# Freed input tiles as output buffers, and a new order for the last head, in a gated attention and MLP backward kernel

## The chip, the cores and the metric

The kernel runs on one core of one Trainium2 chip. The metric is the device time of one execution in microseconds (us). Engines are named as in the profile: PE (TensorE matmul), PEld (its weight load), DVE (VectorE), ACT (ScalarE), POOL (GpSimd) and SP (SyncE, which here only issues transfers). The core has 16 DMA engines, over which a transfer is spread.

## The reference

One decode step of attention over a cache (32 heads, 4096 keys, head size 128) and an MLP are mixed by a gate; the kernel returns the output and the gradients of nine inputs, in bf16.

```python
def _A_ref(x, k_cache, v_cache, wq, wo):           # D = 640
    q = (x @ wq).reshape(B, Sq, H, Dh).transpose(0, 2, 1, 3)
    scores = jnp.einsum("bhqd,bhkd->bhqk", q, k_cache) * (Dh ** -0.5)
    p = _softmax(scores, axis=-1)
    o = jnp.einsum("bhqk,bhkd->bhqd", p, v_cache)
    return o.transpose(0, 2, 1, 3).reshape(B, Sq, H * Dh) @ wo

def _B_ref(x, w1, b1, w2):                         # F = 1728
    h = jnp.einsum("bsd,df->bsf", x, w1) + b1
    sp = jnp.log1p(jnp.exp(-jnp.abs(h))) + jnp.where(h > 0, h, jnp.zeros_like(h))
    return jnp.einsum("bsf,fd->bsd", h * jnp.tanh(sp), w2)

g = _sigmoid((x * gate_w).sum(-1, keepdims=True))
out = g * _A_ref(x, ...) + (1 - g) * _B_ref(B_x, ...)
_out, _vjp = jax.vjp(_f, A_x, A_k_cache, A_v_cache, A_wq, A_wo, B_w1, B_b1, B_w2, gate_w)
return (_out, *_vjp(grad_out))
```

With one query per head, dV of a head is the outer product of p (4096) and do (128), and dK that of ds and the scaled q. So every head reads 1 MB of K and 1 MB of V and writes 1 MB of dV and 1 MB of dK: 128 MB of the 164.6 MB that the kernel moves.

## The kernel before

**Tiles.** A head's K or V is one tile of 128 partitions x 4096 bf16 (`Kn`, `Vn`, 1 MB each; KBUFS = VBUFS = 4 buffers of each). A dV or dK is built in a tile `o_sb` of the same shape, of which there are four. Weights of wq come in pairs of head groups (`wq_p`, 1280 KB), those of wo by group (`wo_g`, 640 KB); w1 and w2 stay in SBUF as a whole (`w1_sb`, `w2_sb`, both `w_sb` in the profile). dWq, dWo, dW1 and dW2 are written over these tiles and stored from there. w2 has 1728 rows: 1664 lie in 13 columns of 128 partitions, the last 64 in column FR, on 64 partitions; its gradient `out_8` is stored in three transfers of the 13 columns (L787) and one of the 64 rows (L788).

**The loop.** `for h in range(H - 1)` (L729) runs heads in a pipeline written out by hand: while head h is finished, K and V of h + 1 are transposed on PE (`k_pe`, `v_pe`, L506) and copied out by ACT (L515, through `ev()`), and scores of h + 1 are made (`k_rows`, `v_rows`). `softmax` finds the maximum, `exps` the exponential (ACT, L566), `pjs` and `zd_mm` the sums, `probs` p and ds (DVE). `dv_out` and `dk_out` build the outer products on DVE in two halves (L589, each 128 x 2048) and store them from SP's queue (L602). `dq_o` has PE read the natural K and V once more (L617) for dq and o of the head; `dqo_red` collects these one head later from what `rw_cp` (ACT) and `x_tr` (PE) bring. It is the last use of Kn and Vn of that head, behind which `load_k(h + 4)` and `load_v(h + 4)` are issued while h + 4 < 32, for the last time at h = 27.

**Groups.** Four heads share a group of weights. At the first head of the next group (hh = 0) the sums of a group are closed: `f_diag`, `f_bc` and `l_dqbf` prepare dq, `l_pe` multiplies it with the transposed wq (`w_pe("q", ...)`, L324, copied by ACT, L330) and o with wo; `f_dwo` writes dWo on ACT (L374), `f_dwq` writes dWq on DVE (L366).

**Queues.** Each engine runs its instructions in the order of the program. All large transfers stand in SP's queue: a store there holds back whatever stands behind it until its data are there. At h = 28 (H - 4) the stores of dW2 are put in, at h = 30 (H - 2) those of db1 and dW1 (L791 to L793). ACT issues four small loads at the start and two stores of `fin_rows` at the end (L906, L908); POOL issues some small ones.

**After the loop** (L840 on) comes head 31: its softmax; `dqo_red(30)`; the sums over three heads of the last group; twenty transposes of wq; `probs`; the second half of dK of 30; `dq_o`; the closing of the group; dWq (DVE, and ACT by `l_dwq`, L361) and its store; dWo on ACT and its store; the end of the small outputs, with dV of 31 in their middle; and dK of 31 as the last thing.

Of the kernel before, what the change touches and what calls it, by code (L numbers as in the profile page):

```python
# [8 lines left out]
ALU = mybir.AluOpType  # L9
# [7 lines left out]
def kernel(  # L17
# [24 lines left out]
    nc = tc.nc  # L42
# [239 lines left out]
    def f_new(g):  # L282
        gp = groups[g]
        gp["o_bf"] = grp_sb.tile([P, G], BF16, name="o_bf", tag="o_bf")
        gp["dq_bc"] = grp_sb.tile([P, GD], BF16, name="dq_bc", tag="dq_bc", bufs=1)
# [9 lines left out]
    def f_bc(g, a=0, b=G):  # L295
        g_bcast(groups[g]["dq_diag"], groups[g]["dq_bc"], a, b)

    def f_o4(g):
        gp = groups[g]
        gp["o4_ps"] = grp([P, G], F32, "o4_ps")  # L300
        nc.tensor.matmul(gp["o4_ps"][:], lhsT=gp["o_sel"][:].rearrange("p h k -> p (h k)"), rhs=res[:],
                         start=True, stop=True)
# [11 lines left out]
    def w_pe(kind, g, k):  # L314
        n = min(TB, G * RC - k * TB)
        tp = tr_ps.tile([P, TB, P], BF16, name="tr", tag="tr")
        for t in range(n):
            if kind == "q":
                hh, c = divmod(k * TB + t, RC)
                src = wqs[g][:, c, hh * Dh:(hh + 1) * Dh]  # L320
            else:
                c, hh = divmod(k * TB + t, G)
                src = wos[g][:, hh, c * P:(c + 1) * P]
            nc.tensor.transpose(tp[:, t, :], src, ident_bf[:])  # L324
        trq.append(lambda: w_ev(kind, g, k, n, tp))
# [27 lines left out]
    def l_add(g, slot, o):  # L353
        ax = groups[g]["ax"]
        if o:
            nc.vector.tensor_tensor(aT_acc[:], aT_acc[:], ax[:, 0, :], ALU.add)
        nc.vector.tensor_copy(dx_parts[:, :, slot], ax[:, 1, :])
# [15 lines left out]
    def f_dwo(g, hh):  # L373
        nc.scalar.activation(wos[g][:, hh, :], da_bc[:], ACT.Copy, scale=groups[g]["o4"][:, hh:hh + 1])  # L374

    def f_dwo_st(g):
        nc.sync.dma_start(dwo4_v[g], wos[g][:])

# [130 lines left out]
    def ev():  # L509
        trq.pop(0)()  # L510
# [27 lines left out]
    def rw_cp(h):  # L538
        rw_sb[h] = small.tile([P, 4, P], F32, name="rw_sb", tag="rw_sb", bufs=1)
        nc.scalar.copy(rw_sb[h][:].rearrange("p t r -> p (t r)"), rw[:])  # L540

    def x_tr(h):
        t = rw_sb.pop(h)
        xs[h] = s_ps.tile([P, 4, P], F32, name="x", tag="x")
        for j in range(4):
            nc.tensor.transpose(xs[h][:, 3 - j, :], t[:, j, :], ident_f[:])  # L546
        v = xs[h][:].rearrange("p t r -> p (t r)").rearrange("p (j u) -> p j u", u=16)
        sd[h] = (v[:, :, 4], v[:, :, 5])
# [19 lines left out]
    def pjs(h):  # L568
        pj = small.tile([P, J], F32, name="pj", tag="pj", bufs=2)
        nc.vector.scalar_tensor_tensor(pj[:], in0=sd[h][1], scalar=1.0, in1=es[h][:],  # L570
                                       op0=ALU.mult, op1=ALU.mult, accum_out=zds[h][:, 1:2])

    def zd_mm(h, mx):
        nc.tensor.matmul(mx[:, P:P + 2], lhsT=ones_f[:], rhs=zds[h][:], start=True, stop=True)  # L574
# [21 lines left out]
    def out_half(w, h, dst, col4, row, k):  # L596
        hh = h % G
        if k == 0:
            o_t[w, h] = outs.tile([P, J, Dh], BF16, name="o_sb", tag="o_sb")
        outer(o_t[w, h], col4, row[:, hh * Dh:(hh + 1) * Dh], k * JH, (k + 1) * JH)  # L600
        if k == 1:
            nc.sync.dma_start(dst[h], o_t.pop((w, h))[:])  # L602
# [4 lines left out]
    def dk_out(h, k):  # L607
        if h >= 0:
            out_half("k", h, dKv, ds4s[h], groups[h // G]["qs_row"], k)
# [12 lines left out]
    def dqo_red(h, x):  # L622
        if h >= 0:
            v = x[:].rearrange("p t r -> p (t r)")[:, 3:3 + 4 * (P - 1)].rearrange("p (s q) -> p s q", q=P - 1)
            nc.vector.tensor_reduce(groups[h // G]["dqo"][:, :, h % G],
                                    v[:, :, 0:P - 1:32].rearrange("p s (i c) -> p i s c", i=2),
                                    axis=AX.XY, op=ALU.add)
# [101 lines left out]
    for h in range(H - 1):  # L729
        g, hh = h // G, h % G  # L730
        nx, pv = g + 1 < NG, g > 0
        k_pe(h + 1, 2)
        ev()
        mx, negM = softmax(h)
        if hh == 3 and nx:
            g_qpair_cp(g + 1)
            g_docol(g + 1)
        dqo_red(h - 1, xs[h])
        k_pe(h + 1, 3)
        ev()  # L740
        exps(h, negM)
        dk_out(h - 1, 1)
        v_pe(h + 1, 0)
        if hh == 2 and nx:
            g_q(g + 1)
        v_pe(h + 1, 1)
        if hh == 3 and nx:
            g_dopair(g + 1)
            g_dopair_cp(g + 1)
        k_rows(h + 1)  # L750
        ev()
        ev()
        pjs(h)
        v_pe(h + 1, 2)
        ev()
        zd_mm(h, mx)
        if hh == 0 and pv:
            f_new(g - 1)
            l_new(g - 1)
            l_dqbf(g - 1, 0, G)  # L760
            f_diag(g - 1)
        elif h >= 2:
            mlp_some(0.9, False)
        v_pe(h + 1, 3)
        ev()
        probs(h, mx)
        if hh == 0 and pv:
            f_o4(g - 1)
            f_o4c(g - 1)
            f_bc(g - 1)  # L770
        dv_out(h, 0)
        k_pe(h + 2, 0)
        dq_o(h)
        v_rows(h + 1)
        rw_cp(h + 1)
        if h + 2 < H:
            ev()
        dv_out(h, 1)
        load_k(h + KBUFS)
        load_v(h + VBUFS)  # L780
        k_pe(h + 2, 1)
        if h + 2 < H:
            ev()
        if h == H - 4:
            assert dw2_next[0] == FCN
            for a, b in W2P:
                nc.sync.dma_start(dw2_v[:, a:b, :], w2_sb[:, a:b, :])  # L787
            nc.sync.dma_start(out_8[FM:F, :], w2_sb[0:FT, FR, :])  # L788
        if h == H - 2:
            assert not mq  # L790
            nc.sync.dma_start(db1_row, dh_bc[0:1, :])  # L791
            nc.sync.dma_start(dw1_v[:, 0:3, :], w1_sb[:, 0:3, :])
            nc.sync.dma_start(dw1_v[:, 3:RC, :], w1_sb[:, 3:RC, :])  # L793
        dk_out(h, 0)
        x_tr(h + 1)
        maxes(h + 1)
        if hh == 0:
            if nx:
                g_new(g + 1)
            if pv:  # L800
                l_pe(g - 1, 0, G)
                wT.pop(("q", g - 1))
                l_add(g - 1, g - 1, True)
                for t in range(G):
                    f_dwo(g - 1, t)
                f_dwo_st(g - 1)
                f_dwq(g - 1, 0)
                f_dwq(g - 1, 1)
        if hh == 1:
            if pv:  # L810
                for c in range(2, RC):
                    f_dwq(g - 1, c)
                f_dwq_st(g - 1)
            if nx:
                w_pe("o", g + 1, 0)
                ev()
                w_pe("o", g + 1, 1)
                ev()
        if hh == 2:
            if g + 2 < NG:  # L820
                load_wo(g + 2)
            if nx:
                w_pe("o", g + 1, 2)
                ev()
                g_do(g + 1)
                g_qcol(g + 1)
                g_qpair(g + 1)
        if hh == 3:
            if g % 2 == 0 and g + 4 <= NG:
                load_wqp(g // 2 + 1)  # L830
            if nx:
                g_qs(g + 1)
                for k in range(NWT):
                    w_pe("q", g, k)
                    ev()
        if h >= 2:
            mlp_some(0.9 if hh < 2 else 1.8)
            dw2_some(2)
# [6 lines left out]
    mx, negM = softmax(h)  # L845
    exps(h, negM)
    dqo_red(h - 1, xs[h])
    f_new(g)
    l_new(g)
    f_diag(g, 0, 3)  # L850
    l_dqbf(g, 0, 3)
    pjs(h)
    zd_mm(h, mx)
    f_bc(g, 0, 3)
    for k in range(NWT):
        w_pe("q", g, k)
        ev()
    l_pe(g, 0, 3)
    probs(h, mx)
    dk_out(h - 1, 1)  # L860
    dq_o(h)
    rw_cp(H)
    l_add(g, g, False)
    x_tr(H)
    dqo_red(h, xs[H])
    f_diag(g, 3, 4)
    l_dqbf(g, 3, 4)
    f_o4(g)
    f_o4c(g)
    f_bc(g, 3, 4)  # L870
    l_pe(g, 3, 4)
    for c in range(RC):
        f_dwq(g, c, 0, 3)
# [1 line left out]
        l_dwq(c, 3, 4)  # L875
    f_dwq_st(g)
    for t in range(G):
        f_dwo(g, t)
    f_dwo_st(g)
    l_add(g, NG, True)  # L880
    fin = const.tile([P, 3 * RC], F32, name="fin")
# [6 lines left out]
                                   accum_out=dgp[:])  # L888
    dg_ps = grp([P, 1], F32, "dg_ps")
    nc.tensor.matmul(dg_ps[:], lhsT=ones_f[:], rhs=dgp[:], start=True, stop=True)  # L890
    dv_out(h, 0)
    dv_out(h, 1)
    dxs = const.tile([P, RC], F32, name="dxs")
    nc.vector.reduce_sum(dxs[:], dx_parts[:], axis=AX.X)
    dz = const.tile([P, 1], F32, name="dz")
# [10 lines left out]
    nc.scalar.dma_start(out0_rows, fin_rows[0:RC, :])  # L906
    nc.gpsimd.dma_start(out1_rows, fin_rows[RC:2 * RC, :])
    nc.scalar.dma_start(out9_rows, fin_rows[2 * RC:3 * RC, :])  # L908
    dk_out(h, 0)
    dk_out(h, 1)  # L910


# [28 lines left out]
```

## Time and profile before

| | us |
|---|---|
| time, median of 3 runs | 406.58 (405.52 to 406.79) |
| the profiled execution, its own time | 406.17 |
| its span, first to last instruction | 404.4 |
| busy: PE, DVE, ACT (share of the span) | 321.1 (79%), 262.7 (65%), 245.3 (61%) |
| moved, mean rate over the span | 164.58 MB, 407 GB/s |
| rate from 10 to 350 | 422 GB/s at a DMA share of 1.01 |
| last stores issued: dK of 30, dWq, dWo, dV of 31, dK of 31 | 383.70, 391.65, 394.52, 394.96, 397.09 |

The span counts from the first to the last instruction of the program; the time of the execution is 1.77 us longer. A row of the page's 40 slices has one digit for each 10.1 us, the busy share in tenths. In the lists of groups, the first number after the bar is the busy time of all instructions of the group, the second the mean of one in ns, and behind the next bar stands the engine's idle time just before them with what ended it. "SPq" and "ACTq" rows are issues of transfers; the time to landing counts from the issue until the last of the 16 DMA engines has reported.

### The profile page before, as it was taken

How to read it: one execution, taken by the hardware profiler on the slowest of the kernel's cores; microseconds unless marked ns; L12 is line 12 of the kernel's file. 1: busy time of each engine (PE TensorE's matmuls, PEld its weight loads, DVE VectorE, ACT ScalarE, POOL GpSimd, SP SyncE). 2: the span in 40 equal slices, each digit the busy share in tenths (PEclk: the TensorE clock that was granted, in tenths of full speed). 3: DMA queues.
4: the chain of work that ended last, by engine and by line, in shares of the span. 5: the costliest groups of instructions: out<-in, count | busy, mean ns of one | idle time of the engine just before them, and what ended most of it. 6: DMA issues, size and time to landing. Idle time of an engine off the chain costs nothing.

```text
span 404.4 us, 8209 instructions
## 1 busy us (share of the span) xinstructions
PE 321.1 (79%) x3210; PEld 223.0 (55%) x3225; DVE 262.7 (65%) x748; ACT 245.3 (61%) x493; POOL 9.7 (2%) x25
## 2 busy tenths in 40 slices
PE   2979989787989988769897979787897979778350
PEld 1556647564766766646565646555564647565230
DVE  2218737767766568757896746775897755758452
ACT  2466757756674656654677767766776656475250
POOL 3000001000000000000002000000000000000000
PEclk9999999989995989898998989968999898889655
DMA  7999999999999999999999999999999999999848
GB/s 276 421 417 423 422 419 408 419 423 423 418 422 420 421 421 425 421 419 427 422 425 426 420 419 425 424 418 425 424 425 425 423 420 427 423 409 389 346 183 336
DMA packets 28684, 164.58 MB, mean 407 GB/s; under 512 B 2917, under 2 KB 3046, under 8 KB 12263
## 3 DMA queue, kind: packets, MB, share of 16 engines
q1 hardware_dynamic: 28338, 164.05, 97.9%
q8 instruction: 25, 0.41, 0.4%
q14 instruction: 13, 0.10, 0.1%
q0 software_dynamic: 256, 0.01, 0.0%
q10 hardware_dynamic: 52, 0.01, 0.0%
HBM read 82.03 MB, written 82.03 MB: 406 GB/s over the span
## 4 chain that ended last, share of the span: by engine, by line
DMA 52%; PE 23%; DVE 15%; ACT 6%; issue 1%; DVEq 0%; SPq 0%; ACTq 0%
DMA out_dram<-o_sb 50%; PE tr L506 8%; DVE o_sb L589 8%; PE rw L529 3%; PE rw L617 3%; DMA wq_p<-in_A_wq_dram 2%; PE tr L324 2%; PE x L546 2%; ACT rw_sb L540 1%; ACT wo_g L374 1%; PE q_ps L211 1%; DVE junk L463 1%; PE h_ps L396 1%; DVE mjunk L485 1%; ACT do_row L266 1%
## 5 line engine op out<-in xcount | busy, mean ns | idle before, releaser
L515 ACT COPY T<-tr 128x512 f32<-128x512 f32 x256 | 138.0, 594 | 56.9 <-PE tr L506 32.1
L589 DVE TENSOR_TENSOR o_sb<-qs_row,ds 128x2048 bf16<-128x2048 bf16 x64 | 78.0, 1220 | 46.5 <-DMA out_dram<-o_sb 46.5
L506 PE MATMUL tr<-ident_f,Vn 128*128 128x128 f32 x512 | 89.0, 311 | 7.0 <-ACT T L515 6.3
L506 PE MATMUL tr<-ident_f,Kn 128*128 128x128 f32 x512 | 86.3, 297 | 5.8 <-DVE rw L499 5.8
L506 PEld LDWEIGHTS tr<-ident_f,Vn 128*128 128x128 f32 x512 | 66.8, 161 | 29.2 <-PE tr L506 12.7
L589 DVE TENSOR_TENSOR o_sb<-do_row,p 128x2048 bf16<-128x2048 bf16 x64 | 75.3, 1218 | 0.0
L506 PEld LDWEIGHTS tr<-ident_f,Kn 128*128 128x128 f32 x512 | 61.1, 150 | 23.8 <-PE rw L617 12.4
L540 ACT COPY rw_sb<-rw 128x512 f32<-128x512 f32 x33 | 19.4, 587 | 45.0 <-PE rw L529 42.8
L617 PE MATMUL rw<-Kn,ds 128*4 128x512 bf16 x256 | 34.7, 394 | 2.9 <-DVE ds L584 2.3
L617 PE MATMUL rw<-Vn,p 128*4 128x512 bf16 x256 | 34.7, 394 | 0.0
L558 PE MATMUL mx<-ident_f,m_s 128*128 128x128 f32 x32 | 10.5, 330 | 27.4 <-DVE m_s L554 27.0
L374 ACT ACTIVATE wo_g<-da_bc,o 128x640 bf16<-128x640 bf16 x32 | 23.9, 816 | 4.7 <-PE ax_ps L350 4.7
L546 PE MATMUL x<-ident_f,rw_sb 128*128 128x128 f32 x132 | 22.1, 291 | 4.7 <-ACT rw_sb L540 1.4
L330 ACT COPY wT<-tr 128x512 f32<-128x512 f32 (+1 forms) x48 | 22.5, 520 | 4.2 <-PE tr L324 4.2
L529 PE MATMUL rw<-T,qz 128*32 128x512 bf16 x256 | 23.3, 445 | 0.0
L558 PEld LDWEIGHTS mx<-ident_f,m_s 128*128 128x128 f32 x32 | 4.7, 146 | 31.4 <-DVE m_s L554 26.3
L546 PEld LDWEIGHTS x<-ident_f,rw_sb 128*128 128x128 f32 x132 | 14.1, 143 | 13.5 <-ACT rw_sb L540 13.5
L529 PE MATMUL rw<-T,doz 128*32 128x512 bf16 x256 | 20.0, 388 | 0.8 <-ACT T L515 0.8
L578 DVE RECIPROCAL rz<-mx 128x1 f32<-128x1 f32 x32 | 5.4, 167 | 23.1 <-PE mx L574 23.0
L617 PEld LDWEIGHTS <-ds 128*4 128x4 bf16 x256 | 9.0, 84 | 17.7 <-DVE ds L584 7.5
L560 DVE TENSOR_REDUCE negM<-mx 128x1 f32<-128x128 f32 x32 | 9.2, 287 | 14.6 <-PE mx L558 14.6
L566 ACT ACTIVATE e_bf<-x,negM 128x32 bf16<-128x32 f32 x32 | 9.4, 293 | 10.9 <-DVE negM L560 6.4
(165 smaller groups left out, 365.3 us busy)
## 6 DMA issues: line engine op xcount, KB each, us to landing
out_dram<-o_sb SPq DMA_DIRECT2D x64, 1024.0 KB, 16.1
Kn<-in_A_k_cache_dram SPq DMA_DIRECT2D x32, 1024.0 KB, 17.1
Vn<-in_A_v_cache_dram SPq DMA_DIRECT2D x32, 1024.0 KB, 18.2
wq_p<-in_A_wq_dram SPq DMA_DIRECT2D x4, 1280.0 KB, 8.7
wo_g<-in_A_wo_dram SPq DMA_DIRECT2D x8, 640.0 KB, 18.0
out_dram<-wo_g SPq DMA_DIRECT2D x8, 640.0 KB, 17.8
out_dram<-wq_p SPq DMA_DIRECT2D x4, 1280.0 KB, 12.3
w_sb<-in_B_w_dram SPq DMA_DIRECT2D x1, 2160.0 KB, 22.6
```

The costliest lines, as they stand in the source:

```text
L330: nc.scalar.copy(wT[kind, g][:, k * TB:k * TB + n, :].rearrange("p a b -> p (a b)").bitcast(F32), tp[:, 0:n, :].rearrange("p a b -> p (a b ...
L374: nc.scalar.activation(wos[g][:, hh, :], da_bc[:], ACT.Copy, scale=groups[g]["o4"][:, hh:hh + 1])
L506: nc.tensor.transpose(tp[:, t, :], words[:, t * P:(t + 1) * P], ident_f[:])
L515: nc.scalar.copy(T[h][:, (3 - c) * (TB // 2):(4 - c) * (TB // 2), :], tp[:])
L529: nc.tensor.matmul(rw[32 * c:32 * (c + 1), :], lhsT=z[:, par, :, :].rearrange("p m u -> p (m u)"), rhs=Tb[:, c, par, :, :], start=first an ...
L540: nc.scalar.copy(rw_sb[h][:].rearrange("p t r -> p (t r)"), rw[:])
L546: nc.tensor.transpose(xs[h][:, 3 - j, :], t[:, j, :], ident_f[:])
L558: nc.tensor.transpose(mx[:, 0:P], dgms.pop(h)[:].to_broadcast([P, P]), ident_f[:])
L560: nc.vector.tensor_reduce(negM[:], mx[:, 0:P], axis=AX.X, op=ALU.max, negate=True)
L566: nc.scalar.activation(es[h][:], sd[h][0], ACT.Exp, bias=negM[:], scale=scale, accum_out=zds[h][:, 0:1])
L589: nc.vector.tensor_tensor(dst[:, a:b, :].rearrange("p j (k t) -> p j k t", t=4), row.rearrange("p (k t) -> p k t", t=4).unsqueeze(1).to_br ...
L617: nc.tensor.matmul(rw[32 * c:32 * c + 4, :], lhsT=c4[:, 4 * jb:4 * jb + 16].rearrange("p (j t) -> p t j", t=4)[:, 0, :], rhs=N[:, jb:jb + ...
```

## The change

Four things are done. First, the last outer products go to tiles of K and V that no load needs any more: dK of heads 28 to 30 to `Kn` buffers, dV of heads 29 to 31 to `Vn` buffers; dK of 31 stays with `o_sb`. Second, for the last head, dV and dK are issued ahead of the sums over its dq and o: the second half of dK of 30 comes right behind `dqo_red`, dV of 31 behind `dq_o`, and the halves of dK of 31 around the closing of dq; the transposes of wq for the last group move into the loop at h = 30 (hh = 2). Third, dWo of the last group is written by DVE (`l_dwo`) instead of ACT. Fourth, the 64 rows that are left of dW2 are stored in six pieces of 1, 2, 3, 4, 5 and 49 rows from ACT's queue, instead of one from SP's.

```diff
+    def l_dwo(hh):
+        nc.vector.tensor_scalar(wos[NG - 1][:, hh, :], da_bc[:], groups[NG - 1]["o4"][:, hh:hh + 1], None, ALU.mult)
+
...
         if k == 0:
-            o_t[w, h] = outs.tile([P, J, Dh], BF16, name="o_sb", tag="o_sb")
+            if w == "k" and H - KBUFS <= h < H - 1:
+                o_t[w, h] = kv_in.tile([P, J, Dh], BF16, name="Kn", tag="Kn")
+            elif w == "v" and h > H - VBUFS:
+                o_t[w, h] = kv_in.tile([P, J, Dh], BF16, name="Vn", tag="Vn", bufs=VBUFS)
+            else:
+                o_t[w, h] = outs.tile([P, J, Dh], BF16, name="o_sb", tag="o_sb")
...
             for a, b in W2P:
                 nc.sync.dma_start(dw2_v[:, a:b, :], w2_sb[:, a:b, :])
-            nc.sync.dma_start(out_8[FM:F, :], w2_sb[0:FT, FR, :])
+            for a, b in ((0, 1), (1, 3), (3, 6), (6, 10), (10, 15), (15, FT)):
+                nc.scalar.dma_start(out_8[FM + a:FM + b, :], w2_sb[a:b, FR, :])
...
         if hh == 2:
             if g + 2 < NG:
                 load_wo(g + 2)
-            if nx:
+            if not nx:
+                for k in range(NWT):
+                    w_pe("q", g, k)
+                    ev()
+            else:
                 w_pe("o", g + 1, 2)
...
     dqo_red(h - 1, xs[h])
+    dk_out(h - 1, 1)
+    pjs(h)
+    zd_mm(h, mx)
     f_new(g)
     l_new(g)
     f_diag(g, 0, 3)
     l_dqbf(g, 0, 3)
-    pjs(h)
-    zd_mm(h, mx)
     f_bc(g, 0, 3)
-    for k in range(NWT):
-        w_pe("q", g, k)
-        ev()
     l_pe(g, 0, 3)
     probs(h, mx)
-    dk_out(h - 1, 1)
     dq_o(h)
     rw_cp(H)
+    dv_out(h, 0)
+    dv_out(h, 1)
+    x_tr(H)
     l_add(g, g, False)
-    x_tr(H)
+    dk_out(h, 0)
     dqo_red(h, xs[H])
     f_diag(g, 3, 4)
     l_dqbf(g, 3, 4)
     f_o4(g)
+    f_bc(g, 3, 4)
+    dk_out(h, 1)
     f_o4c(g)
-    f_bc(g, 3, 4)
     l_pe(g, 3, 4)
...
     for t in range(G):
-        f_dwo(g, t)
+        l_dwo(t)
     f_dwo_st(g)
...
-    dv_out(h, 0)
-    dv_out(h, 1)
...
-    dk_out(h, 0)
-    dk_out(h, 1)
```

## The prediction

> **What bounds the kernel now.** I read the page first, then the chain of waits, then busy time by stage for the last 50 us, the single transfers with their time to landing, and SP's waits.
>
> From the page, the DMA row of the 40 slices and the group that waits longest:
>
> ```profile
> DMA  7999999999999999999999999999999999999848
> ...
> L589 DVE TENSOR_TENSOR o_sb<-qs_row,ds 128x2048 bf16<-128x2048 bf16 x64 | 78.0, 1220 | 46.5 <-DMA out_dram<-o_sb 46.5
> ```
>
> DMA is full until the last three slices; DVE, which multiplies out dK, stands 46.5 us because the four o_sb buffers are still being stored. That invites the reading "free buffers, fill the hole at the end". Busy time by stage says more (window, length, PE, PEld, DVE, ACT, POOL, granted clock, mean share of the 16 DMA engines, GB/s):
>
> ```profile
> 382.10:392.30 10.20, 7.34 (x83) 5.13 (x81) 5.00 (x22) 4.81 (x13) 0.00 (x0) 0.50 0.33 135
> 387.40:392.20 4.80, 2.91 (x34) 2.29 (x34) 3.20 (x18) 2.41 (x7) 0.00 (x0) 0.50 0.06 25
> 392.20:402.80 10.60, 0.53 (x3) 0.25 (x2) 4.80 (x9) 2.55 (x5) 0.56 (x1) 0.50 0.97 384
> ```
>
> A mean share of 0.33 over 10.2 us is a hole of 6.8 us. But 0.06 for 4.8 us is 1/16: **one DMA engine works on alone**, at 25 GB/s, after the other fifteen have run dry. Single issues with their KB and us to landing (the stores issued at 354.23, 383.70 and 397.09, and the dwq store of 391.65) tell how long that engine has been behind:
>
> ```profile
> out_dram<-o_sb SPq DMA_DIRECT2D x1, 1024.0 KB, 13.2
> ...
> out_dram<-o_sb SPq DMA_DIRECT2D x1, 1024.0 KB, 9.1
> ...
> out_dram<-o_sb SPq DMA_DIRECT2D x1, 1024.0 KB, 6.0
> ...
> out_dram<-wq_p SPq DMA_DIRECT2D x1, 1280.0 KB, 4.8
> ```
>
> A store has landed when its last engine is done: 354.23 + 13.2 = 367.4, and 397.09 + 6.0 = 403.1 for the last one. Issued behind the first of them, the last included, are 14,048 KB (dW2 2160, two dWo tiles 640 each, seven dV or dK 1024 each, dW1 2160, dWq 1280), 14.39 MB, or 0.90 MB per engine. In 35.7 us that is **25.2 GB/s, just what the lone engine moves when nothing else runs**. So the last engine has had no pause worth naming since 367; its only one is at 392.3 to 392.5, 0.2 us, when it has finished dK of head 30 and the dWq store, issued at 391.65, has only just come. The hole belongs to the fifteen others.
>
> The second limit is in SP's queue and waits:
>
> ```profile
> 354.23 0.34 SPq L602 DMA_DIRECT2D out_dram<-o_sb  x1
> 354.62 2.63 SPq L787 DMA_DIRECT2D out_dram<-w_sb  x3
> 357.30 1.26 SPq L788 DMA_DIRECT2D out_dram<-w_sb  x1
> 359.77 0.34 SPq L377 DMA_DIRECT2D out_dram<-wo_g  x1
> 362.24 0.33 SPq L602 DMA_DIRECT2D out_dram<-o_sb  x1
> ...
> SPq L602 <- DMA Vn<-in_A_v_cache_dram: 2.1, 1, 2.1
> ```
>
> The store at 362.24 had its data at 358.1 (two products from 354.53 and 356.90, 1.22 each), yet it waited for the landing of a V load it doesn't use. That load, issued at 342.20, is the eighth issue before it. The start shows the same: V of head 1 is issued at 5.66, K of head 0 landed at 0.74 + 4.9 = 5.64; dW1's input at 14.24, V of head 0 landed at 2.22 + 12.0 = 14.22. Each pair is eight issues apart, the first only if the three that ACT issues between are counted. **So at most eight transfers of SP and ACT together are under way, and each issue waits for the eighth before it.**
>
> **The change, part by part.** All sums are against the span of 404.4 us; the profiled execution took 406.17, 1.77 more, and the median of the runs is 406.58.
>
> *Freed K and V tiles.* Six of the last seven outer products no longer take an o_sb buffer. DVE's waits for landed stores from 340 on are 7.5 us in three, of which 0.3 (354.53) and 3.9 (377.08) lie behind the change's first use; so head 31 starts 3.9 us earlier. The new wait is for PE to have read the tile: for head 28 PE's last read ends at 353.1, DVE comes at 354.5: nothing.
>
> *Last head.* Its maximum is known at 379.5 - 3.9 = 375.6, the reduction for dq at 376.1. dK of 30 (one half, 1.22) follows and is issued at about 377.4 instead of 383.70. dV of 31: p and ds took from 379.96 to 382.54; less 3.9, plus the 1.22 put ahead, less the 0.7 of diag and dq_bf put behind, about 379.1; two halves, 381.6 instead of 394.96. dK of 31: one more half beside PE's 1.8 + 0.6 + 1.1 (L617, L540, L546), the sums, the other half: 385.2 instead of 397.09. dWq 387.4, five products of 0.25 and ACT's five of 0.39 in parallel. dWo on DVE: a 128x640 multiply isn't in the trace; 128x512 took 0.30 (L366) and 128x1728 0.67 (L490), so 0.3 to 0.4, four 1.5: issued at 388.6 instead of 394.52. Moving the twenty transposes of wq (2.3 us PE, L324) into head 30 puts them in PE's idle stretch from 373.9. Everything is offered 4 to 13 us sooner.
>
> *What this buys.* The last engine needs dK of 30 at 389.7 (392.8 landing, less 0.4 to land and 2.7 to move 65.5 KB at 25 GB/s), dV at 392.3, dK at 394.9, dWq at 397.4, dWo at 400.7. Before, one of these was late, by 0.2. **Gain: 0.2 us.** The sooner supply only lets the other fifteen finish sooner, and nobody waits for them.
>
> *The rest of dW2.* 64 rows of 1280 B, one SP issue (1.26), become six ACT issues. In the last engine's stretch before it is through dW2 (371.9 to 372.5) four packets between 512 B and 2 KB start, a sixteenth of 64; at 25 GB/s they take 0.05 each, 0.2 us. The pieces of 1, 2, 3, 4, 5 and 49 rows can't go evenly over 16 engines: the last engine's rows go from 4 to between 0 and some 12, -0.2 to +0.4. I take -0.2: a piece of n rows reaches at most n engines, so the five small ones leave most engines without any. The Trainium skill, *DMA: Bandwidth & Descriptors*, "Why a DMA increments its semaphore by 16 and not by 1", says that such a copy uses the lowest-numbered engines, as many as divide its outer size, up to 16: 1 to 5 for the small ones, 7 for 49. By it the sum is -0.2 if the late engine is none of the first seven, +0.2 to +0.4 if it is; no view here numbers engines.
>
> ACT pays for six issues: ACT's cheapest here is 0.27 (L132), its dearest 1.11 (L908), SP's for the same rows 1.26: 1.6 to 7.6 us in front of dWo of group 6 (four of 0.75, L374), the K copies (L515) and the exponential of head 29 (L566), on which PE, then DVE wait. I take 3. Cover: head 29's stores come 3 us late, but were 10 to 13 us ahead of the last engine (landing less issue), and the 3.9 comes back at head 31. So nothing; without that cover it would be 3.
>
> **Sum:** -0.2 - 0.2 = -0.4: span 404.0, time 406.2 against the median.
>
> **Rivals.**
>
> *The mean share binds* (the hole is filled): -6.8 - 0.2 gives a span of 397.4, time 399.6. For it: the 0.33. Against it: the engine at 0.06 and the 25.2 GB/s. The Trainium skill, *Perfetto Trace Analysis*, "What 'DMA-bound' means", allows a bound on specific DMA engines; by that rule filling the mean buys nothing, and the trace agrees.
>
> *A slot held by ACT, at the end.* An SP transfer counted eight behind one of the two ACT stores of fin_rows waits for them. They come some 2.2 behind dWo (the last sums, 391.05 to 395.46, less the 2.3 of dV inside them), at 390.8, plus ACT's 3; small transfers under load took 5.3 (POOL, L907) to 6.5 us to land. Then dWq starts at 399.9 instead of 397.4: 2.5 - 0.4 = +2.1, time 408.7. For it: the new order puts SP's last stores beside fin_rows. Against: in the trace of before no SP issue waited for them. It decides from ACT work over 0.5 us late.
>
> *The six pieces block ACT* (the slower side). Counted right behind dW2's three stores, they wait in turn for the landings of the eight before: the sixth for dW2's first, 354.62 + 14.4 = 369.0. ACT then goes on at 369.4 instead of 355.8, and head 29 and all behind it moves 13.6 us. Dead time starts above some 9.7 (dK of 31 at 385.2 against 394.9). dV of 30 comes at 373.25 + 13.6 = 386.9, and it and all behind it, 8176 KB or 0.523 MB an engine, need 20.8 us at 25.2 GB/s: 387.7 to 408.5, plus 1.6 to the end, 410.1; time 412.3. Against it: if they're counted before SP's stores that ACT overtakes, their eighth has long landed; then SP's V load for head 31 and dK of 27 wait for the pieces instead, with some 1 us to spare. The trace of before, with no ACT issue in the loop, doesn't show which.
>
> **Chances.** Last engine, no new wait 0.54; slot at the end 0.21; ACT blocked 0.13; hole filled 0.10; else 0.02. 0.3% (1.2 us) is what a measurement can tell from no change. Faster: 0.10 and 0.04 of the first case (the late engine at 26 GB/s, as 416/16 at 397.75 to 402.50, on its last 0.37 MB: 0.6 more, and a little besides); slower: 0.13, 0.18 of 0.21, and 0.07 of the first case; same 0.48. The likeliest alone has 405.2 to 407.6. The range 405.0 to 410.5 leaves out the filled hole and most of blocked ACT.
>
> **What would show it.** DMA's share stays near 1 to about 395 and then falls to 0.06 for some us before the end, with the last landing at about 402.7: the main case. A fall to 0 for all engines together: starving, by a slot or by ACT; then SP's or ACT's waits name the transfer. All sixteen ending together near 396: the filled hole, and I'm wrong about the engine. DVE must show no wait for out_dram<-o_sb behind 350.

## The result, and the profile after

The changed kernel takes **406.71 us** (median of 12 runs, 406.22 to 408.51), the kernel before on the same chip 405.81 (12 runs, 405.26 to 406.79): a ratio of **1.0027, interval 1.0014 to 1.0040**. Taken once more beside a later experiment, it is 1.0028 (1.0011 to 1.0045). So the change costs about 1.1 us; the forecast had it 0.4 faster. The time itself lies inside the range on record, on the other side of no change. The profiled execution took 406.80 with a span of 405.0 (before: 406.17 and 404.4).

The page's DMA row and the group of products that waits longest, of the changed kernel:

```profile
DMA  7999999999999999999999999999999999589996
...
L592 DVE TENSOR_TENSOR o_sb<-qs_row,ds 128x2048 bf16<-128x2048 bf16 x58 | 70.8, 1220 | 42.1 <-DMA out_dram<-o_sb 42.1
```

The hole at the end (the 8, 4 and 8 of before) is closed. Another has opened 40 us earlier, the 5 and the 8. The same busy time by stage as before, for three of its windows, and two new ones at the new hole:

```profile
347.00:356.50 9.50, 9.39 (x114) 6.83 (x113) 7.68 (x25) 5.54 (x12) 0.00 (x0) 0.82 0.36 134
360.25:362.75 2.50, 2.50 (x18) 2.06 (x11) 0.82 (x6) 1.57 (x3) 0.00 (x0) 0.59 0.78 233
382.10:392.30 10.20, 3.56 (x35) 2.58 (x35) 6.51 (x28) 2.09 (x7) 0.56 (x1) 0.50 1.02 422
387.40:392.20 4.80, 0.86 (x3) 0.59 (x3) 1.64 (x12) 0.26 (x1) 0.56 (x1) 0.50 1.03 426
392.20:402.80 10.60, 0.00 (x0) 0.00 (x0) 0.00 (x0) 0.00 (x0) 0.00 (x0) 0.50 0.92 376
```

From 382 to 402.8 the transfers run nearly full, and from 392.2 on no compute engine is busy any more: everything is offered in time, as the change wants it. But from 347.0 to 356.5 the mean share is 0.36 where it was 0.99 before, and in the middle of it, 351.25 to 355.0, one engine works alone. The first two windows have lost 6.1 and some 0.55 us of the full share (9.5 x 0.64 and 2.5 x 0.22). What emptied them stands in SP's queue. SP's issues, first of the kernel before and then of the changed one:

```profile
341.70 0.41 SPq L107 DMA_DIRECT2D Kn<-in_A_k_cache_dram  x1
342.20 0.47 SPq L112 DMA_DIRECT2D Vn<-in_A_v_cache_dram  x1
348.11 6.46 SPq L602 DMA_DIRECT2D out_dram<-o_sb  x2
```

```profile
335.73 6.62 SPq L610 DMA_DIRECT2D out_dram<-o_sb  x2
354.65 0.34 SPq L107 DMA_DIRECT2D Kn<-in_A_k_cache_dram  x1
355.18 0.34 SPq L112 DMA_DIRECT2D Vn<-in_A_v_cache_dram  x1
355.61 2.17 SPq L610 DMA_DIRECT2D out_dram<-o_sb  x2
...
364.37 0.33 SPq L380 DMA_DIRECT2D out_dram<-wo_g  x1
```

The last two loads, K and V of head 31, leave 13 us later than before, and dK of head 27 behind them 7.5 us later. SP's waits (total, times, longest) and ACT's issues of the six pieces, both of the changed kernel, say why:

```profile
SPq L107 <- DMA out_dram<-o_sb: 12.2, 1, 12.2
SPq L371 <- DMA out_dram<-fin_rows: 8.1, 1, 8.1
...
SPq L380 <- DMA out_dram<-w_sb: 3.9, 1, 3.9
```

```profile
354.00 0.55 ACTq L797 DMA_DIRECT2D out_dram<-w_sb  x2
354.60 1.31 ACTq L797 DMA_DIRECT2D out_dram<-w_sb  x4
```

The load waits 12.2 us for the landing of a store that it has nothing to do with, dK of head 26. The six pieces are counted ahead of it, so its eighth predecessor is a transfer six places later than before. K leaves when dK of 26 has landed (354.59). The pieces, though counted there, leave only at 354.0, when ACT comes to them: V, behind K, waits for the first of them, which lands at 355.12, and dK of 27 for the second (355.47). In the meantime SP can't go on, and the fifteen engines that are ahead run dry. ACT pays 1.9 us for the six.

A transfer has landed when its last engine reports. The times of the last report of four transfers, taken from the single landing events of the traces (one execution each), show what the late engine loses, and where. The traces don't number the engines; the late one is known by reporting last.

| kernel | K of 31 | V of 31 | dK of 30 | last one of the program |
|---|---|---|---|---|
| before | 359.70 | 362.18 | 392.77 | 403.12 |
| changed | 359.94 | **364.01** | 394.42 | 404.06 |
| changed, rest of dW2 on SP | 359.87 | 362.34 | 393.22 | 402.60 |

The 12.2 us cost the late engine nothing at K: it was busy with older work until 357.4. It loses 1.6 us on V alone, which takes it 4.07 us instead of 2.48. From there the changed kernel stays about 1.4 behind the third one to the end. The fifteen others lose more, and with it their lead: the last report of dV of 27 comes 5.8 us behind the second-latest (357.38 against 351.61), that of V of 31 only 0.05 (364.01 against 363.96).

### The profile page after: what moved, and what is told of

It is laid out like the page before. It is cut to its first block, busy times and chain, and to the rows that moved or that the text cites. A ratio compares the mean times of both kernels' runs of the same rounds, so it can differ in the third digit from the quotient of the medians.

```text
span 405.0 us, 8224 instructions
## 1 busy us (share of the span) xinstructions
PE 320.6 (79%) x3225; PEld 222.7 (55%) x3225; DVE 262.9 (65%) x752; ACT 242.2 (60%) x489; POOL 9.7 (2%) x25
## 4 chain that ended last, share of the span: by engine, by line
issue 42%; DMA 25%; PE 17%; DVE 7%; ACT 4%; POOL 1%; POOLq 0%; SPq 0%; DVEq 0%
DMA out_dram<-o_sb 23%; PE tr L509 7%; DVE o_sb L592 3%; DMA wq_p<-in_A_wq_dram 2%; PE rw L532 2%; PE rw L625 1%; ACT wo_g L374 1%; PE tr L324 1%; PE x L549 1%; PE q_ps L211 1%; DVE junk L466 1%; PE h_ps L399 1%; ACT rw_sb L543 1%; POOL mjunk L473 1%; ACT do_row L266 1%
## 5 line engine op out<-in xcount | busy, mean ns | idle before, releaser
L592 DVE TENSOR_TENSOR o_sb<-qs_row,ds 128x2048 bf16<-128x2048 bf16 x58 | 70.8, 1220 | 42.1 <-DMA out_dram<-o_sb 42.1
L509 PE MATMUL tr<-ident_f,Vn 128*128 128x128 f32 x512 | 90.3, 315 | 8.5 <-ACT T L518 7.8
L509 PEld LDWEIGHTS tr<-ident_f,Vn 128*128 128x128 f32 x512 | 68.1, 163 | 30.1 <-PE tr L509 12.6
L592 DVE TENSOR_TENSOR o_sb<-do_row,p 128x2048 bf16<-128x2048 bf16 x58 | 68.2, 1217 | 0.0
L374 ACT ACTIVATE wo_g<-da_bc,o 128x640 bf16<-128x640 bf16 x28 | 20.9, 816 | 5.1 <-PE ax_ps L350 4.0
L266 ACT CAST do_row<-do_ps 128x512 bf16<-128x512 f32 x8 | 10.3, 1291 | 6.6 <-PE do_ps L263 6.6
```

The lines of the kernel that those rows point to most:

```text
L266: nc.scalar.copy(gp["do_row"][:].rearrange("p (k t) -> p t k", t=G), ps[:].rearrange("p (t k) -> p t k", t=G))
L509: nc.tensor.transpose(tp[:, t, :], words[:, t * P:(t + 1) * P], ident_f[:])
L592: nc.vector.tensor_tensor(dst[:, a:b, :].rearrange("p j (k t) -> p j k t", t=4), row.rearrange("p (k t) -> p k t", t=4).unsqueeze(1).to_br ...
```

## The experiments

The letters in the expectations: **L**, one late engine sets the end, and idle time of the fifteen others is free. **S**, a piece on ACT costs by the place among the eight that it holds in SP's count. **U**, the uneven rows of the pieces on the late engine are the loss. **M**, the mean share binds. **H**, places held by ACT's last stores cost. **R** has two meanings: in the run on POOL's queue, that the uneven pieces slow the loads beside them; in the run with one ACT transfer, that issuing from ACT costs by itself. Kernels of one batch share the runs of the kernel before.

**The rest of dW2 back on SP** (the other parts of the change stay).

```diff
-            for a, b in ((0, 1), (1, 3), (3, 6), (6, 10), (10, 15), (15, FT)):
-                nc.scalar.dma_start(out_8[FM + a:FM + b, :], w2_sb[a:b, FR, :])
+            nc.sync.dma_start(out_8[FM:F, :], w2_sb[0:FT, FR, :])
```

> The changed kernel, with the 64 rows left of dW2 again as one store on SP's queue; freed tiles, new order and dWo on DVE stay. Theory of the last engine (L: one DMA engine never pauses and ends last): 405.2 to 405.8, that is 0.0 to 0.6 below the kernel before; the fifteen others end near 396 and the DMA share stands at 0.06 for 4 us or more before the end, last landing near 402.7. Theory of the mean share (M): all engines end together, about 399. Theory of the slots (S: the six pieces held six of the eight slots from 336 to 355, and that is the changed kernel's whole loss): no hole at 347 to 356, K of head 31 issued near 342 again, and 0.6 to 1.2 below the changed kernel.

405.65 us (11 runs, 405.34 to 406.08) against 406.03, ratio 0.9992 (0.9983 to 1.0001), span 403.9. Busy time in three windows and SP's two loads:

```profile
347.00:356.50 9.50, 9.40 (x115) 6.83 (x113) 7.69 (x25) 5.88 (x13) 0.00 (x0) 0.82 1.00 417
...
391.80:394.00 2.20, 0.00 (x0) 0.00 (x0) 0.00 (x0) 0.00 (x0) 0.00 (x0) 0.50 0.06 26
399.50:402.20 2.70, 0.00 (x0) 0.00 (x0) 0.00 (x0) 0.00 (x0) 0.00 (x0) 0.50 0.06 26
```

```profile
341.93 0.54 SPq L107 DMA_DIRECT2D Kn<-in_A_k_cache_dram  x1
342.56 0.50 SPq L112 DMA_DIRECT2D Vn<-in_A_v_cache_dram  x1
```

The hole at 347 is gone, and the picture of the forecast's main case appears: the fifteen run out, one engine goes on alone at 26 GB/s, the last landing at 402.60 (forecast: 402.7) and the span 403.9 (forecast: 404.0). Freed tiles and new order are worth 0.4 us by the medians, 0.1% at an interval that just holds no change. M, which wanted about 399, is refuted: in the window of the old hole, 382.1 to 392.3, the share goes from 0.33 to 0.74, and the time hardly moves.

**The pieces alone**, in the kernel before.

```diff
-            nc.sync.dma_start(out_8[FM:F, :], w2_sb[0:FT, FR, :])
+            for a, b in ((0, 1), (1, 3), (3, 6), (6, 10), (10, 15), (15, FT)):
+                nc.scalar.dma_start(out_8[FM + a:FM + b, :], w2_sb[a:b, FR, :])
```

> The kernel before, with only the six pieces on ACT's queue added. S: K of head 31 waits for a slot until about 354.6, DMA share about 0.36 from 347 to 356.5, V of head 31 lands near 364.0 instead of 362.2; time 406.5 to 407.5, at or above the changed kernel, since freed tiles and order bring nothing under L. M: the rest of the change was worth several us, so this one is 410 or more.

407.30 us (12 runs, 406.65 to 409.77), ratio 1.0034 (1.0020 to 1.0049). The wait is there without any of the other parts:

```profile
SPq L107 <- DMA out_dram<-o_sb: 11.6, 1, 11.6
```

So the six pieces are the whole loss: 1.0034 alone, 0.9992 without them, beside 1.0027 for all together. (The trace is of an execution of 409.77; only the wait is read from it.)

**The pieces on POOL's queue**, which is not among SP's and ACT's eight.

```diff
-                nc.scalar.dma_start(out_8[FM + a:FM + b, :], w2_sb[a:b, FR, :])
+                nc.gpsimd.dma_start(out_8[FM + a:FM + b, :], w2_sb[a:b, FR, :])
```

> The changed kernel with the six pieces on POOL's queue instead of ACT's. S: POOL's issues are not counted among the eight, so there is no hole at 347 to 356 and the time is that of the run with one store on SP, 405.2 to 405.9. Rival R (the uneven pieces themselves cost: 49 rows on few engines slow the loads beside them): the rate still dips for 2 to 3 us around the pieces, and the time stays near the changed kernel's 406.7.

405.94 us (11 runs, 405.70 to 406.57), ratio 1.0000 (0.9991 to 1.0010). K of 31 leaves at 342.53, and no SP issue waits for a piece. Six pieces as such are not dear; six of them in ACT's queue are. Whether the late engine got the same rows from POOL's queue was not looked at, so this run says nothing of U.

**The rows as one ACT transfer**: one held place instead of six.

```diff
-            for a, b in ((0, 1), (1, 3), (3, 6), (6, 10), (10, 15), (15, FT)):
-                nc.scalar.dma_start(out_8[FM + a:FM + b, :], w2_sb[a:b, FR, :])
+            nc.scalar.dma_start(out_8[FM:F, :], w2_sb[0:FT, FR, :])
```

> The changed kernel with the rest of dW2 as one transfer of 64 rows, still issued by ACT at the same place of the program, instead of six. S (the pieces cost what they hold: each ACT transfer is counted ahead of SP's next ones and keeps one of eight places until it lands): one place is held instead of six, SP's load of K of head 31 leaves at 341.9 to 346 as with the store on SP, there is no stretch with fifteen engines idle at 347 to 356, and the time is that of the store on SP, 405.5 to 406.0. R (what costs is that ACT issues it, or that it goes through a second queue, whatever the number of places): 406.5 to 406.9, as the changed kernel. U (uneven rows on the last engine are the whole loss): also 405.5 to 406.0, but then the hole at 347 to 356 stays.

405.58 us (12 runs, 405.23 to 406.29) against 405.79, ratio 0.9986 (0.9976 to 0.9996). SP's two loads, and the window of the hole:

```profile
342.75 0.34 SPq L107 DMA_DIRECT2D Kn<-in_A_k_cache_dram  x1
345.25 0.34 SPq L112 DMA_DIRECT2D Vn<-in_A_v_cache_dram  x1
```

```profile
347.00:356.50 9.50, 9.39 (x77) 6.83 (x78) 6.86 (x20) 4.80 (x11) 0.00 (x0) 0.70 0.94 393
```

One place delays the loads by 0.8 and 2.7 us against the run with the store on SP, which nobody feels. That ACT issues it is no cost in itself: R falls, S stands.

**The six pieces on SP.**

```diff
-                nc.scalar.dma_start(out_8[FM + a:FM + b, :], w2_sb[a:b, FR, :])
+                nc.sync.dma_start(out_8[FM + a:FM + b, :], w2_sb[a:b, FR, :])
```

> The changed kernel with the six pieces on SP's queue, at their place in SP's own order. Nothing is overtaken any more: K and V of head 31 leave at 342 as before. But each piece now waits, on SP, for the landing of the eighth transfer before it, so the store of dWo's seventh group and dK of head 28 leave at about 371 and 373 instead of 360 and 362. L (one late engine sets the end): that engine has its backlog until about 373 and hardly pauses; the fifteen others stand idle for some 8 to 10 us between 358 and 373; time 405.7 to 406.8, the spread being what the uneven rows give the late engine (5 rows, +0.2) and one latency. M (idle time of the fifteen costs): 409 or more. U (uneven rows alone are the loss of the change): 406.5 to 406.9, whichever queue issues them.

406.54 us (12 runs, 405.49 to 407.33), ratio 1.0008 (0.9995 to 1.0021), same batch as the one before.

```profile
357.61 11.76 SPq L797 DMA_DIRECT2D out_dram<-w_sb  x6
370.79 0.36 SPq L380 DMA_DIRECT2D out_dram<-wo_g  x1
372.84 0.35 SPq L610 DMA_DIRECT2D out_dram<-Kn  x1
```

```profile
363.00:373.00 10.00, 8.74 (x93) 4.95 (x91) 8.75 (x20) 5.74 (x13) 0.00 (x0) 0.96 0.35 141
```

A 6.5 us hole (10 x 0.65) at another place goes with 1 us more than the run beside it (405.58), not 6.5: L again, M's 409 is out. By its time alone, 406.54, this run doesn't tell S from U. Its trace says more: dV of 31 lands last at 395.66, only 0.1 behind the run with one store on SP (395.54), with the hole and the uneven rows behind it. The 1 us comes after that, at dK of 31 (399.06 against 397.96). SP's longest wait for a transfer, in the same trace:

```profile
SPq L610 <- DMA out_dram<-fin_rows: 11.6, 1, 11.6
```

dK of 31 leaves at 395.04, when ACT's store of the final rows has landed, and from 395.0 to 395.5 the mean DMA share is 0.01: here the late engine stands too. In this kernel the slot at the end cost about 1 us, the hole and the rows together 0.1 (one execution each). The trace of this run shows which engine is late: of the piece of five rows, issued at 367.48, four rows had landed by 368.69 and the fifth at 372.98, while the piece of four rows was complete 1.7 us after its issue. The late engine is the fifth that such a transfer uses. The Trainium skill, *DMA: Bandwidth & Descriptors*, "Why a DMA increments its semaphore by 16 and not by 1", has small copies on the lowest-numbered engines; by it this is engine 4. The forecast's "-0.2" had the wrong sign.

**Six pieces with even rows**: still six places on ACT, but four rows on the late engine, as in the single store.

```diff
-            for a, b in ((0, 1), (1, 3), (3, 6), (6, 10), (10, 15), (15, FT)):
+            for a, b in ((0, 4), (4, 8), (8, 12), (12, 16), (16, 20), (20, FT)):
```

> The changed kernel with the rest of dW2 still in six pieces on ACT, but of 4, 4, 4, 4, 4 and 44 rows: a transfer of 4 rows leaves the late engine out (it is the fifth, by the five-row piece on SP whose fifth row landed 4.3 us behind the other four), 44 rows give it 4 rows, as the single store of 64 does. So the six held places stay and the uneven rows go. S (held places): the hole at 347 to 356 stays, K of head 31 leaves at about 354, time 406.3 to 406.8, less than the changed kernel's by at most 0.3 for the five rows. U (the late engine's rows are the loss): the hole stays, time 405.5 to 405.9.

406.36 us (11 runs, 405.86 to 408.47) against 406.12, ratio 1.0007 (0.9995 to 1.0020).

```profile
347.00:356.50 9.50, 8.56 (x117) 6.23 (x115) 8.98 (x27) 6.71 (x14) 0.00 (x0) 1.00 0.35 125
```

```profile
SPq L107 <- DMA out_dram<-o_sb: 12.4, 1, 12.4
```

Hole and wait stay, V of 31 lands last at 363.89, and the time is 0.88 above a single ACT transfer in the same batch (405.48, below, there with the final rows on POOL): U's 405.5 to 405.9 fails, S holds. By the ratio it is still better than the uneven pieces (1.0007 against 1.0027 and 1.0028, in other batches), so the rows may have a share of the loss too; its size is not settled.

**The same uneven pieces one head later**, beside the changed kernel itself, unaltered.

```diff
+        if h == H - 3:
             for a, b in ((0, 1), (1, 3), (3, 6), (6, 10), (10, 15), (15, FT)):
                 nc.scalar.dma_start(out_8[FM + a:FM + b, :], w2_sb[a:b, FR, :])
```

> The changed kernel itself, unaltered, as the yardstick on the same chip for the run beside it: 406.4 to 407.0, a ratio to the kernel before of 1.0014 to 1.004 as it had; K of head 31 leaves at about 354.6 and V of head 31 lands last at about 364.

> The changed kernel with the same six uneven pieces on ACT, issued one head later, so that they are counted behind K and V of head 31 and behind dK of 27 and dV of 28, not ahead of them. S: K and V of head 31 leave at 342 to 343 and V lands last at about 362.2 as in the kernel before; in turn ACT itself waits for the landing of K and V of head 31 before its last two pieces (until about 360 and 362), and SP's first store of dW2 waits for dK of 27 (about 365). L: the fifteen others stand idle some 4 us about 361 to 366, the late engine has dV of 28 until 367 and does not pause, ACT's stop of some 6 us is over before dK of 28 is due at the late engine (374): 405.6 to 406.3, at least 0.4 less than the run beside it, although there are still six held places and the same uneven rows. If a held place costs wherever it is counted, or if the uneven rows are the loss: 406.4 to 407.0, no less than the run beside it; if ACT's stop reaches the stores: 408 or more.

The changed kernel: 406.48 us (11 runs, 406.11 to 409.34), ratio 1.0028 (1.0011 to 1.0045); V of 31 lands last at 364.05. One head later: **406.00** (11 runs, 405.68 to 407.05), 1.0010 (1.0001 to 1.0019); V of 31 lands last at 362.59. SP's issues and the window, of the later pieces:

```profile
342.34 0.47 SPq L107 DMA_DIRECT2D Kn<-in_A_k_cache_dram  x1
342.90 0.53 SPq L112 DMA_DIRECT2D Vn<-in_A_v_cache_dram  x1
348.48 4.96 SPq L610 DMA_DIRECT2D out_dram<-o_sb  x2
365.19 3.40 SPq L795 DMA_DIRECT2D out_dram<-w_sb  x3
```

```profile
358.00:367.00 9.00, 8.62 (x71) 5.90 (x71) 5.97 (x17) 4.62 (x11) 0.00 (x0) 0.81 0.32 132
```

Six held places, uneven rows and a hole as large as that of the changed kernel (9 x 0.68 = 6.1 us), now behind the loads: 0.5 us come back, as much as expected. The expected stop of ACT did not come; it reached the pieces at 364.64, when the loads had landed. So the same hole costs less at this place. It isn't free there: 1.0010 is still some 0.7 us above the 0.9992 of the run without pieces, half of the changed kernel's loss, and the intervals of the two kernels of this batch (1.0001 to 1.0019, 1.0011 to 1.0045) just overlap. One difference shows in the traces: here the fifteen start again on stores, whose packets take 313 to 317 ns per 8 KB on average (366 to 372), there on two loads, the second of them slow (see the end of the next section). Where the 0.7 comes from was not found; in the trace it is there by dV of 31 (396.19 against 395.54).

**Final rows on POOL**, with the rest of dW2 on SP.

```diff
-    nc.scalar.dma_start(out0_rows, fin_rows[0:RC, :])
+    nc.gpsimd.dma_start(out0_rows, fin_rows[0:RC, :])
-    nc.scalar.dma_start(out9_rows, fin_rows[2 * RC:3 * RC, :])
+    nc.gpsimd.dma_start(out9_rows, fin_rows[2 * RC:3 * RC, :])
```

> The changed kernel with the rest of dW2 as one store on SP (as in the first run) and ACT's two stores of the final rows moved to POOL, so that they hold no place and SP's last two stores don't wait for their landing at 393.0 and 393.4. L: the fifteen engines' idle stretch at 389 to 394 fills, dWq and the last dWo are done by the fifteen some us sooner, and the end does not move, since the late engine had no pause: 405.4 to 405.8, within 0.1% of the first run's 405.65. H (the two held places set the end): 403.5 to 404.6.

**405.38 us** (12 runs, 405.00 to 405.99), ratio 0.9985 (0.9976 to 0.9994), span 403.4. The last two stores no longer wait, the fifteen have reported by 396.6, and the end stays:

```profile
396.50:402.00 5.50, 0.00 (x0) 0.00 (x0) 0.00 (x0) 0.00 (x0) 0.00 (x0) 0.50 0.07 27
```

Six us of idle fifteen-sixteenths, paid by nobody; H's 403.5 to 404.6 fails. With **the single ACT transfer and the final rows on POOL** together:

```diff
-            for a, b in ((0, 1), (1, 3), (3, 6), (6, 10), (10, 15), (15, FT)):
-                nc.scalar.dma_start(out_8[FM + a:FM + b, :], w2_sb[a:b, FR, :])
+            nc.scalar.dma_start(out_8[FM:F, :], w2_sb[0:FT, FR, :])
...
-    nc.scalar.dma_start(out0_rows, fin_rows[0:RC, :])
+    nc.gpsimd.dma_start(out0_rows, fin_rows[0:RC, :])
-    nc.scalar.dma_start(out9_rows, fin_rows[2 * RC:3 * RC, :])
+    nc.gpsimd.dma_start(out9_rows, fin_rows[2 * RC:3 * RC, :])
```

> The changed kernel with the rest of dW2 as one ACT transfer and the final rows' stores all on POOL, the two quick forms together. L: no place is held at the end and only one at the start, the late engine has no pause, and the two do not add up, since each alone already leaves that engine without one: 405.2 to 405.6, within 0.1% of either. If held places at the end cost by themselves (H), 0.2 to 0.4 below the form with one ACT transfer: 405.2 or less.

405.48 us (12 runs, 405.07 to 405.92), 0.9984 (0.9974 to 0.9993). The two don't add up, as L has it. With the single ACT transfer alone (0.9986) these are the fastest forms found, and no run tells the three apart: they beat the kernel before by 0.15%, the changed one by about 0.4%.

**Two tries to take rows from the late engine, both misses.** First on the version with the rest of dW2 on SP and the final rows on POOL: the last three stores as 120 and 8 rows.

```diff
+            if (w, h) in (("k", H - 2), ("v", H - 1), ("k", H - 1)):
+                nc.sync.dma_start(dst[h][0:120], o[0:120])
+                nc.sync.dma_start(dst[h][120:P], o[120:P])
```

> The kernel of the first run of this call, with dK of 30 and dV and dK of 31 each stored as 120 and 8 partitions, and the two late ACT stores of fin_rows on POOL's queue (no slot held at the end). 120 rows can go evenly over 15 engines but not over 16. L, if the late engine is the one that such a store leaves out: it has 3 x 65.5 KB or 7.8 us less to move, the others end last near 398 to 399, time 399.5 to 402. L, if the late engine is another: 405.5 to 407. M: 399 with or without the split.

414.20 us (5 runs, 414.06 to 414.76), ratio 1.0200 (1.0183 to 1.0216). The engine that 120 rows leave out was not the late one, and the late one got slower: dV of 31 landed last at 403.93 instead of 395.58. Then, knowing it to be the fifth, dK of 30 as 90 and 38 rows:

```diff
+            if (w, h) == ("k", H - 2):
+                nc.sync.dma_start(dst[h][0:90], o[0:90])
+                nc.sync.dma_start(dst[h][90:P], o[90:P])
```

> The kernel of the run before it, with dK of head 30 stored as 90 rows and 38 rows (two transfers) instead of 128: 90 rows go as 6 to each of fifteen engines, 38 as 19 to each of two, as far as the spread of earlier transfers tells. L with the late engine among those that a transfer of 5 rows uses and not the first two: that engine carries 6 rows of 8 KB instead of 8, about 0.65 us less (8 rows took it 2.6 us), and the time falls to 404.8 to 405.2; the first two engines, 17 rows more, use up the 5 to 6 us by which they were ahead. If the late engine is one of the first two: 410 to 412. C (a store taken apart slows the late engine whatever its rows, as with 120 and 8): 407 or more.

408.75 us (11 runs, 406.60 to 409.07), ratio 1.0054 (1.0037 to 1.0071). The trace is of an execution of 406.63; what the other 2.1 us up to the median are was not traced. The 38 rows did go to two engines, whose parts landed at 392.04 and 393.80. The third-latest report of dV of 31 came at 394.52 where the late engine's had been 395.58, so, if that is the same engine, it did gain 1.1; but the two that carry 19 rows each on top of their 6 came in at 396.18 and 396.28, 9.3 behind the median engine, where 17 extra rows at 0.31 are 5.3. A likely reason shows in the lengths of the 8 KB packets in these traces (ns, of those that start in 380 to 386):

```
kernel                           median   90%   99%
rest on SP, final rows on POOL      309   320   336
dK of 30 as 90 and 38 rows          309   442   836
last three as 120 and 8 rows        309   634   926
```

The median stays. But with rows taken out of their usual engine, the 90% point is 1.4 to 2 times as long and the 99% point 2.5 to 2.8 times. Whether it is the other engines or the second transfer that does it was not tried.

## Why the prediction was wrong, point by point

- **The end is set by one late engine; the hole of before belongs to the others: right.** Three kernels in which the fifteen stand idle for some 6 us, each at another place (358, 363 and 396), lie within 0.15% of the kernel before. What the account leaves out is that the fifteen pay with their lead: at the first two of these holes the last report goes from 5.8 and 6.4 us behind the second-latest to 1.3 and 0.5, and afterwards all sixteen end nearly together. A hole longer than the lead was not tried. With the pieces taken out, span and last landing came within 0.1 us of the main case's. That is partly luck: the forecast has 0.2 in it for the rows, which that run does not save; without it it would have been 404.2 and 402.9.
- **Gain of freed tiles and new order, 0.2 us: right as far as the noise tells.** Measured 0.4 by the medians, at an interval that just holds no change (ratio 0.9992, 0.9983 to 1.0001). The trace of before has the last engine 3.7 us on the dWq store that took 3.1 later, so its pause at 392 was about 0.6, not 0.2.
- **At most eight of SP's and ACT's transfers under way, each issue waiting for the eighth before: right.** All new waits follow from it.
- **The step that failed** is the main case's cost of the six pieces, and in it the sentence under the third rival: "if they're counted before SP's stores that ACT overtakes, their eighth has long landed; then SP's V load for head 31 and dK of 27 wait for the pieces instead, with some 1 us to spare". They are counted so. But six places shift by six the predecessor of everything behind them: the load of K waited 12.2 us, for dK of 26, and V and the stores queued behind it. The margin of 1 us was asked only of the transfers that wait for a piece. The price had been put at nothing; with the pieces' rows (next point) it is 1.4 us (1.0027 less 0.9992 of 406).
- **The pieces' rows, "I take -0.2": wrong sign.** The late engine is the fifth, so the pieces of 5 and 49 rows reach it; they give it 8 rows (one and seven) instead of 4. At 55 ns for a packet of 1280 B that is +0.2. The bounds of -0.2 to +0.4 held it.
- **ACT's six issues: covered, as forecast,** and cheaper than taken (1.9 us, not 3). ACT was not blocked, since the pieces' predecessors had landed.
- **Rival of the slot at the end: it happened and cost next to nothing.** dWq waited 8.1 us for the final rows and left at 394.97 instead of 386.9; the late engine was busy until 399.4. Without that wait: 0.9985 against 0.9992, the intervals overlap. With the six pieces on SP it was dK of 31 that waited, and there it cost about 1 us.
- **What was to show it:** neither picture came in the changed kernel. Its sixteen engines end together, which was put down to a filled hole and an end near 396; they end at 403 to 404, since the hole was not filled but came earlier. The main case's picture is that of the run without the pieces.
- **DVE shows no wait for a landed o_sb store behind 350: right;** its last, 3.1 us, ends at 344.65.

Why V of 31 took the late engine 4.07 us is only half settled. All sixteen engines were slow there (share 0.78, 233 GB/s), fifteen of them restarting from empty on the two loads: packets of 8 KB that start in 360.0 to 362.5 take 430 to 500 ns on average, 309 to 350 with the rest of dW2 on SP. It is so with the even pieces too (435 to 564 from 360.0 to 362.0), so it is not the shape of the pieces. Loads as such are not slower: from 11 to 20 us of the kernel before nothing but loads is under way, and the packets take 309 to 311. Nor is it any start from empty: behind the holes at 358 and 363 the stores take 311 to 335 ns per 8 KB. The slow stretch stands in every trace in which the fifteen start again on these two loads, the pieces alone and the repeated changed kernel among them. What it is in that start, engines in step or something else, was not tried.

## What to carry to other kernels

A small transfer moved to another engine's queue is not off the path: if both queues share a fixed number of open transfers, ask where the new ones are counted, when their engine will really issue them, and which large transfer then waits for a predecessor so many places later. Read a mean DMA share of a sixteenth as one engine alone, ask how long it has been behind, and price every hole by what it does to that engine: it was cheap here while the fifteen others had a lead to lose. To relieve it, hold back neither its loads nor its rows: transfers that put rows on other engines than usual cost more than they saved.

## What the runs showed of the hardware

- **The late engine falls behind slowly.** In the trace of the fastest kernel it lands 0.04 us behind the second-latest at 25 us and 1.35 at 29.2, right behind a 16 KB packet of an instruction queue that took 1.09 at 26.9; others catch up with it in between, and from 200 us on it goes 0.5, 1.8 (250), 4.0 (300), 4.2 (350) to 6.3 (395). Each store adds some 0.1 to 0.2. That it is instruction packets was not tested. The Trainium skill, *DMA: Bandwidth & Descriptors*, "Latency and other measured facts", calls engines 7 and 15 the usually slower ones; here it is the fifth.
- **Behind a hole the engines go on level.** In the kernel before, the last report of dK of 30 is 5.2 behind the second-latest, that of dWq, the next one behind the hole, 0.02. In the changed kernel the late engine ends 0.9 behind the second-latest, instead of 1.2 to 6.3 in the runs without the early hole, and all sixteen are busy until 401; of the 1.7 us by which its V is late (364.01 against 362.34), 1.5 are left at the end (404.06 against 402.60), 0.2 of them for the pieces' rows. With the even pieces 1.6 at V became 0.5 at the end, so not all of such a loss has to stay.
- **Stores split over unusual engines go with longer packets**: 442 and 634 ns instead of 320 at the 90% point. The Trainium skill, same page, "The descriptor swizzle", has each engine of a transfer into 128 partitions on one port of its own. If that holds for stores too, 8 rows from 120 to 127 spread over eight engines would meet on few ports. The packets' lengths agree; the ports themselves no run shows.
